# A decode layer on one core: weights loaded first in full rows, attention one kv head at a time

## The chip, the core and the metric

The kernel runs on one core of one Trainium2 chip. A core has TensorE (PE, which loads a stationary operand and streams a moving one past it), VectorE (DVE), ScalarE (ACT), GpSimd (POOL) and SyncE (SP, which here only issues transfers). Transfers between the chip's memory (HBM) and the on-chip memory (SBUF, 128 partitions) run on 16 DMA engines; products land in PSUM. The metric is the device time of one launch in microseconds (us), the median of several runs. Durations come from a profile of one execution.

## The reference

One token (x, 576 wide, bf16) is normalised. From the normalised row xn two branches are computed, and both are added to x.

```python
x = A_x                                     # 1 x 1 x 576
xn = _layernorm(x)
return x + _A_ref(xn, k_cache, v_cache, wq, wo) + _B_ref(xn, w_in, w_sp, b_sp, w_out)

# A: attention, 32 query heads, 16 kv heads, Dh = 128, the last W = 4096 of 65536 cached keys
q = xn @ wq                                 # wq 576 x 4096
p = softmax(q k^T * Dh ** -0.5)             # two query heads share one kv head
A = (p v).reshape(1, 1, 4096) @ wo          # wo 4096 x 576

# B: gated MLP at sequence length 1
z = gelu(xn @ w_in)                         # w_in 576 x 4608
z1, z2 = z[:2304], layernorm(z[2304:])
B = (z1 * (w_sp * z2 + b_sp)) @ w_out       # w_out 2304 x 576
```

All tensors are bf16. Read from HBM are K and V of 16 heads (1 MiB each, 32 MiB in all), wq and wo (4.7 MB each), w_in (5.3 MB) and w_out (2.7 MB): 51 MB, each byte once.

## The kernel before

**Loads.** All large loads are issued by SP, in program order as far as the scheduler keeps it. K, V, the eight column blocks of wq and the three chunks of w_out share one ring of 11 tiles of 8 KB per partition (`kvpool`); a load into a used tile waits until its last reader is done. `load_kn` and `load_v` (lines 114 to 121) bring a whole head as 128 partitions of 8 KB. The order is K 0 and 1, wq, K 2 and 3, w_in, V 0 to 3, K 4 to 7, w_out, V 4 to 7, K 8 to 15, wo, V 8 to 15. wq comes as blocks of 512 columns, in pieces of 1 KB:

```python
nc.sync.dma_start(t[:, 0:4, :], A_wq[0:512, 512 * bk:512 * (bk + 1)].rearrange("(kt p) c -> p kt c", p=P))
```

**x.** Three small loads on SP, then statistics over partitions with a product with ones (line 91), Ln and Exp on ACT for the reciprocal root (lines 96 and 97), and `xn_col` with xn in five columns (line 99).

**q and z.** The weights are the stationary operand and xn the moving one, one column wide: 32 x 5 products into `qps` (line 251), 36 x 5 into `zps` (line 269). GELU, the second normalisation and the gate follow as small operations on 128 x 36 (lines 278 to 316) and give `hv`.

**Attention in groups of four kv heads** (g = 0 to 3). `transpose_k` (line 124) turns a head's K into kT with 32 transposes on PE (line 131) and four copies of 128 x 1024 out of PSUM, one in three on ACT (line 133), the others on DVE (line 135). `group_scores` puts the four heads of the group on the four column groups of PE (partition rows 0, 32, 64, 96): eight chunks of 512 keys, four products each (line 148), and one Exp over 98 rows (line 156). `group_ptrans` turns the probabilities back with 32 transposes (line 170) and four copies (line 173). `group_pv` runs, head after head, 32 products of 128 x 2 by 128 x 128 on that head's column group (line 185), then scales (line 194), transposes and copies into `oT_all`.

**Output.** Products with one column of `hv` or `oT_all` as the stationary operand and rows of w_out (line 343) or wo (line 210) as the moving one, 512 and 64 columns, on two column groups. At the end wo's products of groups 0 and 1 come before V of group 2, and so on; lines 375 to 379 give this order. The sum is added to x on one partition (line 387) and stored.

The framework's scheduler chooses the order of each engine's instructions from the program order, and sets all semaphores.

Of the kernel before, what the change touches and what calls it, by code (L numbers as in the profile page):

```python
# [12 lines left out]
AXX = mybir.AxisListType.X  # L13

# [8 lines left out]
NFT = F // 128  # L23
NT = W // 128
NKC = W // 512
NGRP = 4
# [4 lines left out]
DEV_ATTN_ONLY = False  # L31
# [3 lines left out]
def kernel(  # L35
# [19 lines left out]
    ps_s = ctx.enter_context(tc.tile_pool(name="ps_s", bufs=1, space=bass.MemoryType.PSUM))  # L55
    ps_t = ctx.enter_context(tc.tile_pool(name="ps_t", bufs=4, space=bass.MemoryType.PSUM))
    ps_o = ctx.enter_context(tc.tile_pool(name="ps_o", bufs=1, space=bass.MemoryType.PSUM))
    ps_early = tc.alloc_tile_pool(name="ps_early", bufs=1, space=bass.MemoryType.PSUM)
    kvpool = ctx.enter_context(tc.tile_pool(name="kvpool", bufs=11))
    ktpool = ctx.enter_context(tc.tile_pool(name="ktpool", bufs=4))  # L60
    ppool = ctx.enter_context(tc.tile_pool(name="ppool", bufs=2))

    x_flat = A_x.flatten_outer_dims()

    ones_f = const.tile([P, P], FP32, name="ones_f")
    nc.vector.memset(ones_f[:], 1.0)
    ident = const.tile([P, P], BF16, name="ident")
    make_identity(nc, ident[:])
    eps_t = const.tile([P, 1], FP32, name="eps_t")
    nc.vector.memset(eps_t[:], EPS)  # L70

    xcol_bf = const.tile([P, 5], BF16, name="xcol_bf")
    nc.sync.dma_start(xcol_bf[:, 0:4], x_flat[0, 0:512].rearrange("(t p) -> p t", p=P))
    nc.sync.dma_start(xcol_bf[0:64, 4:5], x_flat[0, 512:576].rearrange("(t p) -> p t", p=64))
    x_row = const.tile([1, D], BF16, name="x_row")
    nc.sync.dma_start(x_row[:], x_flat)
    x_col = const.tile([P, 5], FP32, name="x_col")
    nc.vector.memset(x_col[:], 0.0)
    nc.vector.tensor_copy(x_col[:, 0:4], xcol_bf[:, 0:4])
    nc.vector.tensor_copy(x_col[0:64, 4:5], xcol_bf[0:64, 4:5])  # L80

    stat2 = const.tile([P, 2], FP32, name="stat2")
    nc.vector.reduce_sum(stat2[:, 0:1], x_col[:], axis=AXX)
    junk5 = work.tile([P, 5], FP32, name="junk5")
    nc.vector.tensor_tensor_reduce(  # L85
        out=junk5[:], in0=x_col[:], in1=x_col[:], scale=1.0, scalar=0.0,
        op0=ALU.mult, op1=ALU.add, accum_out=stat2[:, 1:2],
    )
    early_ps = ps_early.tile([P, 80], FP32, name="early_ps")
    XS = 68  # L90
    nc.tensor.matmul(early_ps[:, XS:XS + 2], lhsT=ones_f[:], rhs=stat2[:], start=True, stop=True)  # L91
    mv = const.tile([P, 4], FP32, name="mv")
    nc.vector.tensor_scalar_mul(mv[:, 0:2], early_ps[:, XS:XS + 2], 1.0 / D)
    nc.vector.tensor_mul(mv[:, 2:3], mv[:, 0:1], mv[:, 0:1])
    nc.vector.tensor_sub(mv[:, 2:3], mv[:, 1:2], mv[:, 2:3])
    nc.scalar.activation(mv[:, 2:3], mv[:, 2:3], ACT.Ln, bias=eps_t[:, 0:1])
    nc.scalar.activation(mv[:, 3:4], mv[:, 2:3], ACT.Exp, scale=-0.5)
    xn_col = const.tile([P, 5], BF16, name="xn_col")
    nc.vector.tensor_scalar(out=xn_col[:], in0=x_col[:], scalar1=mv[:, 0:1], scalar2=mv[:, 3:4],
                            op0=ALU.subtract, op1=ALU.mult)  # L100

    oT_all = const.tile([P, HQ], BF16, name="oT_all")
    sps = [ps_s.tile([P, 512], FP32, name=f"sps{b}") for b in range(2)]
    for b in range(2):
        nc.vector.memset(sps[b][:], 0.0)
    ops = ps_o.tile([P, DH], FP32, name="ops")
    nc.vector.memset(ops[:], 0.0)

    kn_tiles: dict = {}
    kT_tiles: dict = {}  # L110
    v_tiles: dict = {}
    state = {"sps": 0, "cp": 0}

    def load_kn(j):
        kn = kvpool.tile([P, NT, DH], BF16, name=f"kn{j}", tag="kv")
        nc.sync.dma_start(kn[:], A_k_cache[0, j, SK - W:SK, :].rearrange("(p t) d -> p t d", p=P))
        kn_tiles[j] = kn

    def load_v(j):
        v_sb = kvpool.tile([P, NT, DH], BF16, name=f"v_sb{j}", tag="kv")  # L120
        nc.sync.dma_start(v_sb[:], A_v_cache[0, j, SK - W:SK, :].rearrange("(p t) d -> p t d", p=P))
        v_tiles[j] = v_sb

    def transpose_k(j):
        kn = kn_tiles.pop(j)
        kT = ktpool.tile([P, NT, P], BF16, name=f"kT{j}", tag="kT")
        for q in range(NT // 8):
            tps = ps_t.tile([P, 8, P], BF16, name=f"ktps{j}_{q}", tag="tps")
            for s8 in range(8):
                t = 8 * q + s8  # L130
                nc.tensor.transpose(tps[:, s8, :], kn[:, t, :], ident[:])  # L131
            if state["cp"] % 3 == 2:
                nc.scalar.copy(kT[:, 8 * q:8 * q + 8, :], tps[:, :, :])  # L133
            else:
                nc.vector.tensor_copy(kT[:, 8 * q:8 * q + 8, :], tps[:, :, :])
            state["cp"] += 1
        kT_tiles[j] = kT

    def group_scores(g):
        p_sb = ppool.tile([P, NT, P], BF16, name=f"p_sb{g}", tag="p_sb")  # L140
        acc = work.tile([P, NKC], FP32, name=f"acc{g}", tag="acc")
        for kc in range(NKC):
            sp = sps[state["sps"] % len(sps)]
            state["sps"] += 1
            for i in range(4):
                j = 4 * g + i
                h0 = 2 * j
                nc.tensor.matmul(  # L148
                    sp[32 * i:32 * i + 2, :],
                    lhsT=q_bf[:, h0:h0 + 2],  # L150
                    rhs=kT_tiles[j][:, 4 * kc:4 * kc + 4, :],
                    start=True,
                    stop=True,
                    tile_position=(0, 32 * i),
                )
            nc.scalar.activation(  # L156
                p_sb[0:NR, 4 * kc:4 * kc + 4, :], sp[0:NR, :], ACT.Exp, scale=SCALE,
                accum_out=acc[0:NR, kc:kc + 1],
            )
        for i in range(4):  # L160
            kT_tiles.pop(4 * g + i)
        return p_sb, acc

    def group_ptrans(g, p_sb):
        ptsb = ppool.tile([P, NT, 8], BF16, name=f"ptsb{g}", tag="ptsb")
        for ti in range(NT // 8):
            ptps = ps_t.tile([P, 8, P], BF16, name=f"ptps{g}_{ti}", tag="tps")
            for s8 in range(8):
                t = 8 * ti + s8
                nc.tensor.transpose(ptps[:, s8, 0:NR], p_sb[0:NR, t, :], ident[0:NR, 0:NR])  # L170
            src = ptps[:, :, :].rearrange("p t (q r) -> p t q r", q=4)[:, :, :, 0:2]
            dst = ptsb[:, 8 * ti:8 * ti + 8, :].rearrange("p t (q r) -> p t q r", q=4)
            nc.vector.tensor_copy(dst, src)
        return ptsb

    def group_pv(g, ptsb, acc):
        asum = work.tile([P, 1], FP32, name=f"asum{g}", tag="asum")
        nc.vector.reduce_sum(asum[0:NR, :], acc[0:NR, :], axis=AXX)
        rs = work.tile([P, 1], FP32, name=f"rs{g}", tag="rs")
        nc.vector.reciprocal(rs[0:NR, :], asum[0:NR, :])  # L180
        for i in range(4):
            j = 4 * g + i
            vj = v_tiles.pop(j)
            for tt in range(NT):
                nc.tensor.matmul(  # L185
                    ops[32 * i:32 * i + 2, :],
                    lhsT=ptsb[:, tt, 2 * i:2 * i + 2],
                    rhs=vj[:, tt, :],
                    start=(tt == 0),
                    stop=(tt == NT - 1),  # L190
                    tile_position=(0, 32 * i),
                )
        on_sb = work.tile([P, DH], BF16, name=f"on_sb{g}", tag="on_sb")
        nc.vector.tensor_scalar_mul(on_sb[0:NR, :], ops[0:NR, :], rs[0:NR, :])
        otps = ps_t.tile([P, 8, P], BF16, name=f"otps{g}", tag="tps")
        nc.tensor.transpose(otps[:, 0, 0:NR], on_sb[0:NR, :], ident[0:NR, 0:NR])
        src = otps[:, 0, :].rearrange("p (q r) -> p q r", q=4)[:, :, 0:2]
        dst = oT_all[:, 8 * g:8 * g + 8].rearrange("p (q r) -> p q r", q=4)
        nc.vector.tensor_copy(dst, src)  # L199

    NCH0, NCH1 = 512, D - 512
    out_ps = [None, None]
    out_tp = [(0, 0), (0, 32)]
    out_splits = [(0, NCH0), (NCH0, NCH1)]

    def emit_wo_mms(h_lo, h_hi, wo_sb, last):
        for h in range(h_lo, h_hi):
# [28 lines left out]
    for kt in range(4):  # L236
        nc.sync.dma_start(win_sb[kt][:], B_w_in[kt * P:(kt + 1) * P, :])
# [187 lines left out]
```

## Time and profile before

| | |
|---|---|
| median of 3 runs | 151.73 us (151.55 to 153.25) |
| span of the profiled execution | 149.2 us; its own time is not listed beside it |
| mean granted TensorE clock | 0.874 |
| PE busy | 120.2 us (81%) |
| DVE, ACT busy | 41.4 us, 47.2 us |
| bytes on SP's queue | 50.96 MB, 17252 packets |
| mean rate over the span | 343 GB/s |

Busy time of PE is modelled and pipelined products overlap in it, so 81% is not a measure of how near PE is to its peak. The page cuts the span into 40 slices of 3.7 us, with the rate of the transfers in each. A stage table gives the same for stretches of one's own choice: busy time of each engine (instructions in brackets), granted clock as a share of full speed, share of the time that the DMA engines were busy, and GB/s. The chain that ended last is followed back from the end, and names at each step what released it. In a group's row stand line, engine, operation, output<-input, shapes, count, then busy us and mean ns, then idle time of the engine ahead of it and what ended it.

### The profile page before, as it was taken

What the parts mean: (1) busy time and instruction counts of PE and PEld (TensorE: products, weight loads), DVE (VectorE), ACT (ScalarE), POOL (GpSimd) and SP (SyncE); (2) the same over time, 40 slices, a digit from 0 to 9 for tenths busy, and PEclk for the clock granted to TensorE, in tenths of its full rate; (3) what the DMA queues carried; (4) which work ended last, traced back from release to release, by engine and by line L of the source; (5) the groups of instructions that cost most, each with busy time, mean ns of one, the idle gap of its engine ahead of it and who ended that gap; (6) DMA issues with size and microseconds to landing.
All of it is one profiled execution on the core that took longest, in us unless ns stands there. A gap on an engine that the chain in (4) does not pass through costs nothing. (4 is left out here: it accounts for less than half of the span.)

```text
span 149.2 us, 3824 instructions
## 1 busy us (share of the span) xinstructions
PE 120.2 (81%) x1728; PEld 94.1 (63%) x1728; DVE 41.4 (28%) x109; ACT 47.2 (32%) x94; POOL 1.9 (1%) x8
## 2 busy tenths in 40 slices
PE   0188566799840799998999999899799999969881
PEld 0187455677320699898876479686389546957850
DVE  3247000026210000431775010476169420010012
ACT  3414000024930000440558510346967970000000
POOL 4000000000000000000000000000000000000000
PEclk9999855558995555579999999999999999999999
DMA  2789999999999999999999999999999999999200
GB/s 10 277 336 308 282 285 290 366 422 418 420 348 189 402 422 422 413 413 362 359 415 417 420 415 420 415 422 413 365 357 357 373 415 415 422 413 411 121 0 0
DMA packets 17556, 51.20 MB, mean 343 GB/s; under 512 B 1858, under 2 KB 12868, under 8 KB 12868
## 3 DMA queue, kind: packets, MB, share of 16 engines
q1 hardware_dynamic: 17252, 50.96, 92.8%
q8 instruction: 13, 0.21, 0.6%
q0 software_dynamic: 288, 0.00, 0.2%
q14 instruction: 3, 0.02, 0.0%
HBM read 50.96 MB, written 0.00 MB: 342 GB/s over the span
## 5 line engine op out<-in xcount | busy, mean ns | idle before, releaser
L269 PE MATMUL early_ps<-xn_col,win_sb_242 128*128 128x1 bf16 x36 | 6.0, 166 | 4.0 <-DMA win_sb_242<-in_B_w_in_dram 4.0
L210 PE MATMUL out_t<-wo_sb,oT_all 128*1 128x64 bf16 (+1 forms) x64 | 8.2, 285 | 0.5 <-DVE oT_all L199 0.5
L269 PE MATMUL early_ps<-xn_col,win_sb_243 64*128 64x1 bf16 x36 | 6.6, 183 | 2.4 <-DMA win_sb_243<-in_B_w_in_dram 2.4
L148 PEld LDWEIGHTS <-q_bf 128*2 128x2 bf16 x128 | 3.8, 80 | 7.2 <-issue 4.0
L185 PEld LDWEIGHTS <-ptsb_546 128*2 128x2 bf16 x128 | 8.2, 96 | 0.0
L185 PEld LDWEIGHTS <-ptsb_1627 128*2 128x2 bf16 x128 | 6.9, 84 | 1.0 <-issue 0.7
L185 PEld LDWEIGHTS <-ptsb_1874 128*2 128x2 bf16 x128 | 6.9, 84 | 1.0 <-issue 0.7
L133 ACT COPY kT_422<-ktps_0_423 128x1024 bf16<-128x1024 bf16 x1 | 1.0, 1012 | 18.3 <-PE ktps_0_423 L131 18.3
L269 PE MATMUL early_ps<-xn_col,win_sb_239 128*128 128x1 bf16 x36 | 6.6, 185 | 0.0
L185 PEld LDWEIGHTS <-ptsb_1243 128*2 128x2 bf16 x128 | 6.5, 84 | 0.1
L269 PEld LDWEIGHTS <-win_sb_242 128*128 128x128 bf16 x36 | 3.7, 104 | 4.1 <-DMA win_sb_242<-in_B_w_in_dram 4.1
L285 ACT ACTIVATE th_gelu<-u_gelu 128x36 f32<-128x36 f32 x1 | 0.2, 232 | 19.1 <-DVE u_gelu L283 19.1
L269 PE MATMUL early_ps<-xn_col,win_sb_240 128*128 128x1 bf16 x36 | 5.9, 165 | 0.0
L269 PE MATMUL early_ps<-xn_col,win_sb_241 128*128 128x1 bf16 x36 | 5.9, 165 | 0.0
L269 PEld LDWEIGHTS <-win_sb_243 64*128 64x128 bf16 x36 | 3.7, 102 | 3.0 <-DMA win_sb_243<-in_B_w_in_dram 2.5
L278 DVE COPY zsb<-early_ps 128x36 f32<-128x36 f32 x1 | 0.2, 194 | 17.5 <-PE early_ps L269 17.5
L210 PEld LDWEIGHTS <-oT_all 128*1 128x1 bf16 x64 | 2.6, 81 | 3.8 <-DVE oT_all L199 0.8
L131 PEld LDWEIGHTS <-kn_122 128*128 128x128 bf16 x32 | 3.1, 137 | 2.8 <-DMA kn_122<-in_A_k_cache_dram 2.8
L258 DVE CAST q_bf<-early_ps 128x32 bf16<-128x32 f32 x1 | 0.2, 192 | 15.3 <-PE early_ps L251 15.3
L91 PE MATMUL early_ps<-stat_100,ones_f 128*128 128x2 f32 x2 | 0.6, 363 | 4.6 <-DVE stat_100 L85 4.6
L269 PEld LDWEIGHTS <-win_sb_240 128*128 128x128 bf16 x36 | 4.1, 115 | 0.0
L269 PEld LDWEIGHTS <-win_sb_239 128*128 128x128 bf16 x36 | 3.7, 103 | 0.5
(337 smaller groups left out, 299.9 us busy)
## 6 DMA issues: line engine op xcount, KB each, us to landing
wo_sb<-in_A_wo_dram SPq DMA_DIRECT2D x4, 1152.0 KB, 17.6
win_sb_239<-in_B_w_in_dram SPq DMA_DIRECT2D x1, 1152.0 KB
win_sb_240<-in_B_w_in_dram SPq DMA_DIRECT2D x1, 1152.0 KB, 14.6
win_sb_241<-in_B_w_in_dram SPq DMA_DIRECT2D x1, 1152.0 KB, 15.8
win_sb_242<-in_B_w_in_dram SPq DMA_DIRECT2D x1, 1152.0 KB
kn_122<-in_A_k_cache_dram SPq DMA_DIRECT2D x1, 1024.0 KB, 5.6
kn_124<-in_A_k_cache_dram SPq DMA_DIRECT2D x1, 1024.0 KB, 8.9
kn_150<-in_A_k_cache_dram SPq DMA_DIRECT2D x1, 1024.0 KB, 9.2
```

Of the source, the lines that this page charges most:

```text
L91: nc.tensor.matmul(early_ps[:, XS:XS + 2], lhsT=ones_f[:], rhs=stat2[:], start=True, stop=True)
L131: nc.tensor.transpose(tps[:, s8, :], kn[:, t, :], ident[:])
L133: nc.scalar.copy(kT[:, 8 * q:8 * q + 8, :], tps[:, :, :])
L148: nc.tensor.matmul(sp[32 * i:32 * i + 2, :], lhsT=q_bf[:, h0:h0 + 2], rhs=kT_tiles[j][:, 4 * kc:4 * kc + 4, :], start=True, stop=True, til ...
L185: nc.tensor.matmul(ops[32 * i:32 * i + 2, :], lhsT=ptsb[:, tt, 2 * i:2 * i + 2], rhs=vj[:, tt, :], start=(tt == 0), stop=(tt == NT - 1), t ...
L210: nc.tensor.matmul(out_ps[n], lhsT=oT_all[:, h:h + 1], rhs=wo_sb[:, h, c0:c0 + cw], start=st if DEV_ATTN_ONLY else False, stop=(last and h ...
L258: nc.vector.tensor_copy(q_bf[:], qps)
L269: nc.tensor.matmul(zps[:, t:t + 1], lhsT=win_sb[kt][0:kp, t * P:(t + 1) * P], rhs=xn_col[0:kp, kt:kt + 1], start=(kt == 0), stop=(kt == 4),)
L278: nc.vector.tensor_copy(zsb[:], zps)
L285: nc.scalar.activation(th[:], u[:], ACT.Exp, scale=-2.0 * GELU_C)
```

## The change

Nearly the whole body is rewritten.

- **Order of loads.** wq, then w_in, each as four tiles of 128 partitions and a fifth for the remaining 64 rows; then K 0, K 1, V 0, K 2, V 1 and so on, eleven at once and two more per step of the head loop; after K and V w_out (two tiles) and wo (chunks of 8, 8, 8, 5 and 3 heads) into the space that wq and w_in held. A weight tile t holds rows 4p + t, in full rows: 8 KB (wq) or 9.2 KB (w_in) per partition; the last 64 rows are cut in two halves, so that they too fill 128 partitions. w_out has nine successive rows per partition. wo keeps its rows of 1152 bytes. The ring holds K and V alone.
- **Order of instructions.** PE and SP are under a manual schedule: they run in program order. DVE, ACT and POOL stay with the scheduler. x is loaded on ACT's queue.
- **q and z.** xn is stationary (`xz`, one column of 32 filled), the weights are moving: 40 products of 512 columns for q, 60 of 384 for z, each four on the four column groups. The rows are turned into columns with 8 and 9 small products.
- **Statistics.** The reciprocal root is a power on POOL in place of Ln and Exp on ACT.
- **Attention, one kv head per step.** A head's 4096 keys are split over the four column groups: eight score products in two banks, two Exp, eight transposes of the probabilities, 32 PV products that alternate over the column groups. The sum over the four groups is done by two float32 products: `den` (the denominator) and `ot` (the output column). Step j has the transposes of K j, those of the probabilities of j - 1, the output column of j - 2, the scores of j, PV of j - 1, then two loads. Copies of kT go to DVE, the third of four to ACT.
- **Output.** w_out and wo are multiplied after the head loop, each row in four pieces of 144 columns on the four column groups; x is added on four partitions.

The diff, cut to its core (removed lines as in the listing above; what is left out are declarations, the small operations of the GELU and the renamed constants):

```diff
+KV_BUFS = 11
+WO_CHUNKS = (8, 8, 8, 5, 3)
...
+    nc.scalar.dma_start(xa[:], x_flat[0, 0:512].rearrange("(p t) -> p t", t=4))
...
+    def wrows(src, t):
+        return src[0:512, :].rearrange("(p t) c -> p t c", t=4)[:, t, :]
+
+    def whalf(src):
+        return src[512:576, :].rearrange("m (c j) -> (m c) j", c=2)
...
+    kv_order = [("k", 0)]
+    for j in range(1, HKV):
+        kv_order += [("k", j), ("v", j - 1)]
+    kv_order.append(("v", HKV - 1))
+    kv_order.reverse()
...
+    order = tc.manual_schedule(engines={PE, SP})
+    ctx.enter_context(order)
+
+    for t in range(4):
+        nc.sync.dma_start(wq_sb[t][:], wrows(A_wq, t))
+    nc.sync.dma_start(wq_h[:], whalf(A_wq))
+    for t in range(4):
+        nc.sync.dma_start(win_sb[t][:], wrows(B_w_in, t))
+    nc.sync.dma_start(win_h[:], whalf(B_w_in))
+    load_next(KV_BUFS)
...
+    def mean_rstd(stat_t, n, nm):
+        nc.tensor.matmul(ops[:, MS:MS + 2], lhsT=ones_f[:], rhs=stat_t[:], start=True, stop=True)
...
+        nc.gpsimd.tensor_tensor(mv[:, 3:4], mv[:, 2:3], mhalf[:], ALU.pow)
+        return mv
...
+    for t in range(5):
+        for b in range(2):
+            for i in range(4):
+                if t < 4:
+                    lhsT, rhs = xz[:, t, :], wq_sb[t][:, QC * i + 512 * b:QC * i + 512 * (b + 1)]
+                else:
+                    c0 = QC * (i % 2) + 512 * b
+                    lhsT, rhs = xz[:, 4 + i // 2, :], wq_h[:, c0:c0 + 512]
+                nc.tensor.matmul(
+                    sps[b][32 * i:32 * i + 32, :], lhsT=lhsT, rhs=rhs,
+                    start=(t == 0), stop=(t == 4), tile_position=(0, 32 * i),
+                )
...
+    w2pool = tc.alloc_tile_pool(name="w2pool", bufs=1, reuse_waits="tile")
...
+            for i in range(4):
+                c = 4 * b + i
                 nc.tensor.matmul(
+                    sps[b][32 * i:32 * i + 2, :], lhsT=q_bf[:, 2 * j:2 * j + 2],
+                    rhs=parts[c // 2][:, 512 * (c % 2):512 * (c % 2) + 512],
+                    start=True, stop=True, tile_position=(0, 32 * i),
                 )
...
+        for b in range(2):
+            for s in range(4):
+                for i in range(4):
+                    nc.tensor.matmul(
+                        ops[32 * i:32 * i + 2, 0:DH], lhsT=pt[:, 4 * b + s, i, :],
+                        rhs=v[:, 4 * (4 * b + i) + s, :],
+                        start=(b == 0 and s == 0), stop=(b == 1 and s == 3), tile_position=(0, 32 * i),
+                    )
...
+    for j in range(HKV + 2):
+        if j < HKV:
+            transpose_k(j)
+        if j == 0:
+            gz = z_columns()
+        if j == 1:
+            z_gate(*gz)
+        if 1 <= j <= HKV:
+            transpose_p(j - 1)
+        if j >= 2:
+            o_columns(j - 2)
+        if j < HKV:
+            scores(j)
+        if 1 <= j <= HKV:
+            pv(j - 1)
+        load_next(2)
+        if j == 10:
+            for i in range(2):
+                nc.sync.dma_start(
+                    wout_sb[i][:], B_w_out[ZC * i:ZC * (i + 1), :].rearrange("(p t) n -> p t n", t=9))
+            h0 = 0
+            for n, c in enumerate(WO_CHUNKS):
+                nc.sync.dma_start(
+                    wo_sb[n][:], A_wo[DH * h0:DH * (h0 + c), :].rearrange("(h d) n -> d h n", d=DH))
+                h0 += c
...
+    def project(lhsT, rhs, first, last):
+        for g in range(4):
             nc.tensor.matmul(
+                outp[32 * g:32 * g + 1, :], lhsT=lhsT, rhs=rhs[:, OC * g:OC * (g + 1)],
+                start=first, stop=last, tile_position=(0, 32 * g),
             )
```

More of the change, by code (lines that the diff above doesn't have):

```diff
@@ L58 @@
[L58 to L61, printed above, removed]
-    x_flat = A_x.flatten_outer_dims()
[L65 to L87, printed above, removed]
-    )
-    early_ps = ps_early.tile([P, 80], FP32, name="early_ps")
@@ L90 @@
[L90 to L107, printed above, removed]
+    wpool = tc.alloc_tile_pool(name="wpool", bufs=1)
@@ new lines @@
+    sps = [ps_fix.tile([P, 512], FP32, name=f"sps{b}") for b in range(2)]
+    ops = ps_fix.tile([P, 512], FP32, name="ops")
+    outp = ps_fix.tile([P, OC], FP32, name="outp")
+    nc.vector.memset(ops[:], 0.0)
+    nc.vector.memset(outp[:], 0.0)
+    x_col = const.tile([P, 6], FP32, name="x_col")
+    nc.vector.tensor_copy(x_col[:, 0:4], xa[:])
+    nc.vector.tensor_scalar(out=x_col[:, 4:6], in0=mask2[:], scalar1=xd[:, 0:1], scalar2=None, op0=ALU.mult)
+    stat = const.tile([P, 2], FP32, name="stat")
@@ new lines @@
+    qrow = const.tile([P, QC], BF16, name="qrow")
+    nc.vector.tensor_copy(qrow[:, 0:512], sps[0][:])
+    nc.scalar.copy(qrow[:, 512:1024], sps[1][:])
+    MQ = 288
+    for hh in range(8):
+        nc.tensor.matmul(
+            ops[:, MQ + 4 * hh:MQ + 4 * hh + 4], lhsT=qrow[:, DH * hh:DH * (hh + 1)],
+            rhs=ident[:, 0:P:32], start=True, stop=True,
+        )
+    q_bf = const.tile([P, HQ], BF16, name="q_bf")
+    nc.vector.tensor_copy(
+        q_bf[:].rearrange("p (i h) -> p i h", i=4),
+        ops[:, MQ:MQ + HQ].rearrange("p (h i) -> p i h", i=4),
+    )
@@ new lines @@
+    zps = [ps_t.tile([P, 512], FP32, name=f"zps{b}", tag="tps") for b in range(3)]
+    for t in range(5):
+        for b in range(3):
+            for i in range(4):
+                if t < 4:
+                    lhsT, rhs = xz[:, t, :], win_sb[t][:, ZC * i + ZB * b:ZC * i + ZB * (b + 1)]
+                else:
+                    c0 = ZC * (i % 2) + ZB * b
+                    lhsT, rhs = xz[:, 4 + i // 2, :], win_h[:, c0:c0 + ZB]
+                nc.tensor.matmul(
+                    zps[b][32 * i:32 * i + 32, 0:ZB], lhsT=lhsT, rhs=rhs,
+                    start=(t == 0), stop=(t == 4), tile_position=(0, 32 * i),
+                )
@@ L139, in group_scores @@
[L139 to L144, printed above, removed]
+        parts = []
+        for c in range(4):
+            tps = ps_t.tile([P, 8, P], BF16, name=f"ktps{j}_{c}", tag="tps")
+            for s in range(8):
+                nc.tensor.transpose(tps[:, s, :], kn[:, 8 * c + s, :], ident[:])
+            kT = ktpool.tile([P, 1024], BF16, name=f"kT{j}_{c}", tag="kT")
+            src = tps[:].rearrange("p a b -> p (a b)")
+            if c == 2:
+                nc.scalar.copy(kT[:], src)
+            else:
+                nc.vector.tensor_copy(kT[:], src)
+            parts.append(kT)
@@ L201 @@
[L201 to L207, printed above, removed]
-            for n, (c0, cw) in enumerate(out_splits):
-                st = (DEV_ATTN_ONLY and h == 0 and n >= 0)
-                nc.tensor.matmul(
-                    out_ps[n],
-                    lhsT=oT_all[:, h:h + 1],
-                    rhs=wo_sb[:, h, c0:c0 + cw],
-                    start=st if DEV_ATTN_ONLY else False,
-                    stop=(last and h == HQ - 1),
-                    tile_position=out_tp[n],
-                )
@@ L393, with transpose_p @@
-    nc.sync.dma_start(out.flatten_outer_dims()[:, :], res[:])
-    ps_out.release()
+                p_sb[0:NR, b, :], sps[b][0:NR, :], ACT.Exp, scale=SCALE, accum_out=acc[0:NR, b:b + 1],
+            )
+        asum = work.tile([P, 1], FP32, name=f"asum{j}", tag="asum")
+        nc.vector.reduce_sum(asum[0:NR, :], acc[0:NR, :], axis=AXX)
+        p_tiles[j] = (p_sb, asum)
+    def transpose_p(j):
+        p_sb, asum = p_tiles.pop(j)
+        ptps = ps_t.tile([P, 8, P], BF16, name=f"ptps{j}", tag="tps")
+        for b in range(2):
+            for s in range(4):
+                nc.tensor.transpose(
+                    ptps[:, 4 * b + s, 0:NR], p_sb[0:NR, b, 128 * s:128 * (s + 1)], ident[0:NR, 0:NR])
+        pt = work.tile([P, 8, 4, 2], BF16, name=f"pt{j}", tag="pt")
+        nc.vector.tensor_copy(pt[:], ptps[:].rearrange("p t (q r) -> p t q r", q=4)[:, :, :, 0:2])
+        pt_tiles[j] = pt
+        den = ps_t.tile([P, 512], FP32, name=f"den{j}", tag="tps")
+        nc.tensor.matmul(den[0:NR, 0:1], lhsT=mx_f[0:NR, 0:NR], rhs=asum[0:NR, :], start=True, stop=True)
+        rden = work.tile([P, 1], FP32, name=f"rden{j}", tag="rden")
+        nc.vector.reciprocal(rden[0:NR, :], den[0:NR, 0:1])
+        rd_tiles[j] = rden
```

392 lines of the change are left out of this document (162 added, 230 removed).

## The prediction

> **What bounds the kernel now.** I read the page's slices first, then a table of stages, then the chain that ended last. The page shows an almost full transfer queue:
>
> ```profile
> span 149.2 us, 3824 instructions
> PE 120.2 (81%) x1728; PEld 94.1 (63%) x1728; DVE 41.4 (28%) x109; ACT 47.2 (32%) x94; POOL 1.9 (1%) x8
> GB/s 10 277 336 308 282 285 290 366 422 418 420 348 189 402 422 422 413 413 362 359 415 417 420 415 420 415 422 413 365 357 357 373 415 415 422 413 411 121 0 0
> q1 hardware_dynamic: 17252, 50.96, 92.8%
> wo_sb<-in_A_wo_dram SPq DMA_DIRECT2D x4, 1152.0 KB, 17.6
> ```
>
> The reader sees 50.96 MB on one queue and a rate with plateaus and dips. The table of stages gives them (stretch, length, busy time of PE, PEld, DVE, ACT, POOL, granted clock, DMA share, GB/s):
>
> ```profile
> 14.00:26.00 12.00, 7.82 (x116) 6.38 (x116) 0.51 (x1) 0.00 (x0) 0.00 (x0) 0.65 1.11 284
> 30.00:42.00 12.00, 11.21 (x124) 7.30 (x125) 3.79 (x9) 7.41 (x18) 0.00 (x0) 0.81 1.01 420
> 44.00:46.00 2.00, 0.00 (x0) 0.00 (x0) 0.00 (x0) 0.00 (x0) 0.00 (x0) 0.70 0.99 154
> 46.00:48.00 2.00, 0.18 (x1) 0.10 (x1) 0.00 (x0) 0.00 (x0) 0.00 (x0) 0.50 1.01 214
> 48.00:50.00 2.00, 0.63 (x10) 0.58 (x11) 0.00 (x0) 0.00 (x0) 0.00 (x0) 0.50 0.94 336
> 106.00:118.00 12.00, 11.93 (x191) 9.41 (x190) 8.15 (x17) 9.20 (x20) 0.00 (x0) 1.00 1.08 357
> 120.00:136.00 16.00, 14.75 (x213) 10.39 (x212) 1.41 (x7) 2.45 (x8) 0.00 (x0) 1.00 1.01 418
> ```
>
> wq in 1 KB pieces (14 to 26 us) moves at 284 GB/s, wo in rows of 1152 bytes (106 to 118) at 357, w_in and K and V with 8 or 9 KB per partition at 420 and 418. From 44 to 50 us the stream falls off while PE does nothing: the last of w_in is awaited and K and V tiles hold the ring. Against 418 these three rows lose 2.5 us. The end, from the chain and the timeline, and the stretch in which the stream dies out:
>
> ```profile
> 121.08 20.30 DMA v_sb_1241<-in_A_v_cache_dram
> 141.43 1.96 PE ops L185 x32
> 146.22 0.68 DVE res L387
> 147.16 0.26 SPq L393 DMA_DIRECT2D out_dram<-res  x1
> 135.00:140.00 5.00, 5.00 (x87) 4.61 (x86) 0.00 (x0) 0.00 (x0) 0.00 (x0) 1.00 0.77 318
> 140.00:142.00 2.00, 1.47 (x28) 1.28 (x25) 0.00 (x0) 0.00 (x0) 0.00 (x0) 1.00 0.05 20
> ```
>
> The chain's last long piece is a transfer; what follows the last V tile takes 149.2 - 141.4 = 7.8 us. In the last two rows 1.63 MB pass, 3.9 us of work at 418, but the tile is there only at 141.4: the 16 engines do not finish together, which costs 141.4 - 138.9 = 2.5 us. So the kernel is bound by bytes, at three rates, with a hole and a long tail.
>
> **The change part by part: the stream.** The bytes stay 50.96 MB, of which wo is 4 x 1152 KB = 4.72 MB. wq becomes pieces of 8 KB (four tiles) and 4 KB, w_in 9.2 and 4.6 KB, w_out 10.4 KB; wo keeps 1152 bytes. The start:
>
> ```profile
> 0.74 0.42 SPq L73 DMA_DIRECT2D xcol_bf<-in_A_x_dram  x1
> 2.34 0.35 SPq L116 DMA_DIRECT2D kn_122<-in_A_k_cache_dram  x1
> 3.00:3.50 0.50, 0.00 (x0) 0.00 (x0) 0.00 (x0) 0.00 (x0) 0.00 (x0) 1.00 0.93 69
> 3.51 0.17 DVE L79 CAST x_col<-xcol_bf 128x4 f32<-128x4 bf16 x1 [1.21 <-DMA xcol_bf<-in_A_x_dram]
> 7.68 0.29 DVE L99 TENSOR_SCALAR xn_col<-x_col,mv 128x5 bf16<-128x5 f32 x1 [1.88 <-ACT mv L97]
> bsp<-in_B_b_sp_dram POOLq DMA_DIRECT2D x1, 0.5 KB, 6.9
> ```
>
> Three x loads stand ahead of the first K on SP; moved to ACT's queue, they let SP issue wq at 0.74 instead of 2.34, and bytes flow, 0.9 us after issue as now, from 1.7 us. Full rate 46.24 MB / 418 = 110.6 us; wo 4.72 / 357 = 13.2 us. The skew at the end I keep at 2.5 us. The same sum for the present stream (3.2 start, 16.6 for wq, 20.7 for w_out and wo, 93.0 for the rest, 2.5 hole, 2.5 skew = 138.5) falls 2.9 us short of 141.4; much of that is the uneven start with narrow wq pieces, so I carry 1.0 us over. The last chunk of wo lands at 1.7 + 110.6 + 13.2 + 2.5 + 1.0 = 129.0 us. No run shows wq or w_in with one row in four per tile (32 KB and 37 KB apart); their rate is bounded by 284 and 420, and I take 418, as the pieces are as long as K's.
>
> **Is the stream ever stopped?** SP's order is fixed: ten weight loads, eleven K and V tiles, then two per step of the head loop, each waiting for a tile that PE has read; behind a waiting load stand all later ones, w_out and wo too. The twelfth K/V tile needs head 0's transposes. Weights end at about 1.7 + 1.0 + 10.03 MB / 418 = 26.7 us, the eleven tiles (2.51 us each) at 54; PE can start head 0 near 30. That is 24 us of slack, and each later load has it too unless PE falls behind by as much.
>
> **PE per head.** Rows that give its work (start, length):
>
> ```profile
> 32.70 1.06 PE L131 MATMUL ktps_2_443<-ident,kn_150 128*128 128x128 bf16 x8
> 33.55 1.06 PE L131 MATMUL ktps_3_453<-ident,kn_150 128*128 128x128 bf16 x8
> 111.40 0.45 PE ktps_0_1710 L131 x8
> 87.45 6.59 PE ops L185 x128
> 105.42 0.39 PE sps_115 L148 x4
> 105.80 0.28 PE ptps_0_1628 L170 x4
> L91 PE MATMUL early_ps<-stat_100,ones_f 128*128 128x2 f32 x2 | 0.6, 363 | 4.6 <-DVE stat_100 L85 4.6
> L133 ACT COPY kT_422<-ktps_0_423 128x1024 bf16<-128x1024 bf16 x1 | 1.0, 1012 | 18.3 <-PE ktps_0_423 L131 18.3
> L135 DVE COPY kT_1043<-ktps_3_1074 128x1024 bf16<-128x1024 bf16 x1 | 0.7, 693 | 0.1
> L156 ACT ACTIVATE p_sb_1585<-sps_115 98x512 bf16<-98x512 f32 x4 | 2.4, 598 | 0.0
> L194 DVE TENSOR_SCALAR on_sb_2232<-ops,rs_2102 98x128 bf16<-98x128 f32 x1 | 0.4, 352 | 9.6 <-PE ops L185 9.6
> ```
>
> At full clock: K transposes 32 in 1.8 us (8 in 0.45); two packs of four scores 0.8; eight P transposes 0.56; PV 32 x 51.5 ns = 1.65 (128 in 6.59), now alternating over the four column groups, which can only shorten it if four overlap as the scores do (four in 0.39), to 0.4 at least; the two new float32 products (`den`, `ot`) between 0 and the 0.6 us of a float32 pair, I take 0.3 each. Sum 5.4 us; 4.15 with full overlap, 6.0 with neither gain; I take 4.8, the middle of the first two. A head's 2 MiB take 5.02 us. The four copies lie beside it: DVE 3 x 0.69 + 0.35 and some small ones, about 3 us; ACT 1.0 + 2 x 0.8 = 2.6. The scores of a head wait for its last copy, about 0.8 us after the last transpose; the P transposes of the head before, `den` and `ot` (1.2 us) stand between on PE and cover it. If DVE ran late by more than 0.4 us, PV and all heads behind it would move by the rest, in every step. PE starts at half clock (eight transposes in 0.85) and pays for the z columns and the z gate: PE's order is fixed, so the gate's product waits for GELU with head 0's P transposes queued behind it. I allow 13 us for the first two steps, to 43 us; 14 steps of 4.8 end at 110, two closing steps at 113. K and V are then all there (107), w_out lands near 114, and the 200 products of 144 columns wait for wo. q and z, 100 products in 25 packs of four where 340 stood, run beneath the weight stream: the half-clock start makes a pack some 0.5 us (an estimate: twice 0.39 for 512 columns, less for 384), 13 us in all, of which only w_in's last piece is left when the weights end. That holds if xn is there by about 15 us. The slowest small load above took 6.9 us and x's statistics 4.5 (3.5 to 8.0), so I expect xn by 12. They now end in a GpSimd power that stands in no row: the ACT pair it replaces lies within those 4.5 us, so it gains at most about 2 and is covered up to 3 us more; beyond that PE starts later by the rest, and 113 against the 129 of wo still hides 10 us of it.
>
> **The tail.** After wo's last three heads 12 products of 144 columns are left: 12 x 0.114 (half-clock PV, 1.4 us) at most, 0.3 if they overlap; I take 0.8. The sum over four rows of 144 is like the 98x128 one above, 0.37, hops 0.2, and the output from issue to end 149.2 - 147.16 = 2.04. Together 3.4 us, against 7.8. Span 129.0 + 3.4 = 132.4 us. The median of the runs, 151.73, is 2.5 us above the profiled span of 149.2; with the same surroundings the time is **135.0 us**, 11% below. A difference within 2% counts as no change.
>
> **A rule of the Trainium skill against this.** TensorE: Matmul & The Clock Gate, Part 4, says that transposes do not count as PE work for the clock gate, so that full clock does not engage for them. Here transposes in a row took 0.45 us per eight at 111 us, against 0.85 at 33 us, so the trace disagrees. By that rule the time would be rival 3's.
>
> **Rivals.** (1) PE becomes the bound. With the 5.4 us above plus 0.2 of waits per step: 43 + 14 x 5.6 + 3 + 200 x 58 ns (one product's spacing, as an unpacked transpose) + 2.6 = 139 us, time 141. For it: PE was busy 14.75 of 16 us in the stage from 120 us; against: that stage holds products that do not alternate column groups, and busy time counts pipelined products one over the other. 13%.
> (2) The weight rows miss the plateau. At 357 GB/s wq and w_in take 28.1 us instead of 24.0, time 139; at 284, 35.3, time 146. For it: 1 KB and 1152 bytes differ little, yet 284 and 357 differ much, so more than the length may count in wq's spaced rows. 11%. DMA: Bandwidth & Descriptors, Specifications, has line rate from 512 bytes on; by it 1 KB pieces would already be at the plateau and something else slows wq. The 357 at 1152 bytes speaks against the rule.
> (3) Slower: the clock. PE is now idle or lightly busy for 30 us and then waits in every step. If transposes ran at half clock throughout, a step is 4.8 + 1.8 + 0.56 = 7.2 us: 43 + 14 x 7.2 + 3 + 11.6 + 2.6 = 161, time 163. It decides from a step of 6.6 us on (155 us). That the clock can stay low while PE is busy:
>
> ```profile
> 50.00:60.00 10.00, 10.00 (x163) 9.12 (x160) 0.00 (x0) 0.00 (x0) 0.00 (x0) 0.50 1.01 419
> ```
>
> These were 128x1 products; at 33 us transposes themselves opened it within about 4 us. 4%.
> (4) The change does not do what it says: the load order stops somewhere, as at 44 us now, for 2.5 to 5 us: time 138 to 140. 4%.
>
> **How the numbers follow.** My forecast has 68%; the rest above. Downward, no skew and wo at 418 would save 4.4, to 130.6; two of these are unlikely together, so the low end is 131. The high end, 142, takes in rival 1, rival 4 and rival 2 at 357; left out are rival 3, rival 2 at 284 and a little more, some 12 in 100. Faster by over 2% (below 148.7) 0.93; within 2% 0.03; slower 0.04.
>
> **What would show it.** After: 410 to 420 GB/s from 2 us to about 115 without a hole, then 357; the first head's transposes near 30 us; PE waiting on K tiles by the later heads and on wo at the end; after the last transfer under 4 us. Wrong if wq's stretch stays below 400 GB/s, if SP waits for PE mid-stream, or if PE still works through heads when wo has landed.

## The result and the profile after

The changed kernel takes 136.56 us (median of 4 runs, 136.48 to 136.64) where the kernel before takes 152.23 (4 runs, 151.55 to 153.25). The ratio is 0.897, 95% interval 0.892 to 0.902: 10% faster. The forecast was 135.0 in a range of 131 to 142. The page after, the same rows as were read before:

```profile
span 134.7 us, 3783 instructions
PE 87.2 (65%) x1674; PEld 70.5 (52%) x1674; DVE 51.1 (38%) x173; ACT 38.9 (29%) x84; POOL 3.6 (3%) x11
GB/s 119 348 307 416 425 430 421 410 425 416 423 416 423 418 416 418 406 423 411 421 418 411 414 414 423 418 418 411 418 423 414 422 422 414 360 358 356 311 81 3
DMA packets 11145, 51.21 MB, mean 380 GB/s; under 512 B 1400, under 2 KB 5496, under 8 KB 5752
q1 hardware_dynamic: 10520, 50.96, 94.4%
q8 instruction: 13, 0.21, 0.7%
```

The same 50.96 MB go in 10520 packets instead of 17252. The hole in mid-stream and the stretch at 284 GB/s are gone; wo's step to some 358 GB/s remains, now at the end, and the first slices (3.4 us each), in which wq is loaded, are uneven. As a table of stages (stretch, length, busy PE, PEld, DVE, ACT, POOL, granted clock, DMA share, GB/s):

```profile
2.00:10.00 8.00, 0.00 (x0) 0.00 (x0) 0.79 (x5) 1.05 (x1) 1.48 (x4) 1.00 0.95 318
6.00:8.00 2.00, 0.00 (x0) 0.00 (x0) 0.03 (x1) 0.00 (x0) 0.00 (x0) 1.00 0.87 246
10.00:112.00 102.00, 79.57 (x1468) 64.61 (x1472) 48.44 (x161) 37.62 (x83) 1.10 (x2) 0.88 1.01 418
116.00:126.00 10.00, 3.50 (x100) 2.88 (x100) 0.00 (x0) 0.00 (x0) 0.00 (x0) 0.50 1.08 357
126.00:130.00 4.00, 1.70 (x52) 1.48 (x52) 0.00 (x0) 0.00 (x0) 0.00 (x0) 0.50 0.63 209
```

For 102 us the stream runs at 418 GB/s without a stop; from 2 to 10 us, the larger part of wq's stretch (its last load lands at 16.0), it has 318. The chain's end and the store, from the timeline:

```profile
120.82 9.72 DMA wo_308<-in_A_wo_dram
130.58 0.56 PE outp L405 x11
131.16 0.31 DVE res L422
131.50 0.65 SPq L423 DMA_DIRECT2D out_dram<-res  x1
```

The last transfer is there at 130.5 us (before: 141.4), and 134.7 - 130.5 = 4.2 us follow (before: 7.8). Of the 14.5 us between the spans, 10.9 are the stream and 3.6 the tail.

### The profile page after: what moved, and what is told of

It reads as the page before. It is cut to its first block, busy times and chain, and to the rows that moved or that the text cites. A ratio compares the mean times of both kernels' runs of the same rounds, so it can differ in the third digit from the quotient of the medians.

```text
span 134.7 us, 3783 instructions
## 1 busy us (share of the span) xinstructions
PE 87.2 (65%) x1674; PEld 70.5 (52%) x1674; DVE 51.1 (38%) x173; ACT 38.9 (29%) x84; POOL 3.6 (3%) x11
## 2 busy tenths in 40 slices
DMA packets 11145, 51.21 MB, mean 380 GB/s; under 512 B 1400, under 2 KB 5496, under 8 KB 5752
## 3 DMA queue, kind: packets, MB, share of 16 engines
q1 hardware_dynamic: 10520, 50.96, 94.4%
HBM read 50.96 MB, written 0.00 MB: 378 GB/s over the span
## 4 chain that ended last, share of the span: by engine, by line
DMA 60%; SPq 15%; PE 14%; DVE 5%; ACT 3%; issue 1%; ACTq 0%
DMA kn_1315<-in_A_k_cache_dram 16%; DMA kn_859<-in_A_k_cache_dram 15%; SPq L398 15%; DMA kn_108<-in_A_k_cache_dram 14%; DMA wq_88<-in_A_wq_dram 8%; DMA wo_308<-in_A_wo_dram 7%; PE ops L252 3%; PE sps_146 L326 1%; ACT p_583 L331 1%; ACT p_469 L331 1%; PE ktps_0_312 L309 1%; ACT p_697 L331 1%; PE ktps_0_399 L309 1%; PE ktps_1_323 L309 1%; PE ktps_2_421 L309 1%
## 5 line engine op out<-in xcount | busy, mean ns | idle before, releaser
L405 PEld LDWEIGHTS <-oT_all 128*1 128x1 bf16 x128 | 3.7, 114 | 8.6 <-issue 8.6
L169 PE MATMUL ops<-stat,ones_f 128*128 128x2 f32 x2 | 0.6, 362 | 10.4 <-DVE stat L162 10.4
L237 PEld LDWEIGHTS <-xz 128*32 128x32 bf16 x60 | 2.1, 117 | 9.5 <-issue 8.4
L243 DVE COPY zrow<-zps_232 128x384 f32<-128x384 f32 x1 | 0.6, 558 | 11.4 <-PE zps_232 L237 11.4
L252 PEld LDWEIGHTS ops<-id4f,zrow 128*128 128x128 f32 x18 | 4.4, 336 | 0.0
L309 PEld LDWEIGHTS <-kn_108 128*128 128x128 bf16 x32 | 3.3, 149 | 2.0 <-DMA kn_108<-in_A_k_cache_dram 2.0
L252 PE MATMUL ops<-id4f,zrow 128*128 128x4 f32 x18 | 4.4, 376 | 0.0
L405 PEld LDWEIGHTS <-hv 128*1 128x1 bf16 x72 | 1.8, 108 | 3.7 <-issue 3.7
L309 PEld LDWEIGHTS <-kn_110 128*128 128x128 bf16 x32 | 3.3, 148 | 0.8 <-issue 0.8
L208 PEld LDWEIGHTS <-xz 128*32 128x32 bf16 x40 | 1.3, 131 | 3.8 <-issue 2.1
L309 PEld LDWEIGHTS <-kn_1201 128*128 128x128 bf16 x32 | 1.8, 98 | 2.5 <-DMA kn_1201<-in_A_k_cache_dram 2.5
L405 PE MATMUL outp<-wout_310,hv 128*1 128x144 bf16 x36 | 1.2, 320 | 2.2 <-DMA wout_310<-in_B_w_out_dram 2.2
L405 PE MATMUL outp<-wo_305,oT_all 128*1 128x144 bf16 x32 | 1.1, 319 | 2.2 <-DMA wo_305<-in_A_wo_dram 2.2
L405 PE MATMUL outp<-wo_306,oT_all 128*1 128x144 bf16 x32 | 1.1, 318 | 2.2 <-DMA wo_306<-in_A_wo_dram 2.2
L309 PEld LDWEIGHTS <-kn_745 128*128 128x128 bf16 x32 | 1.8, 98 | 1.2 <-DMA kn_745<-in_A_k_cache_dram 1.2
L405 PE MATMUL outp<-wo_304,oT_all 128*1 128x144 bf16 x32 | 1.1, 320 | 2.0 <-DMA wo_304<-in_A_wo_dram 2.0
L309 PEld LDWEIGHTS <-kn_1429 128*128 128x128 bf16 x32 | 1.8, 98 | 1.2 <-DMA kn_1429<-in_A_k_cache_dram 1.2
L309 PEld LDWEIGHTS <-kn_973 128*128 128x128 bf16 x32 | 1.8, 98 | 1.2 <-DMA kn_973<-in_A_k_cache_dram 1.2
```

The lines of the kernel that those rows point to most:

```text
L169: nc.tensor.matmul(ops[:, MS:MS + 2], lhsT=ones_f[:], rhs=stat_t[:], start=True, stop=True)
L208: nc.tensor.matmul(sps[b][32 * i:32 * i + 32, :], lhsT=lhsT, rhs=rhs, start=(t == 0), stop=(t == 4), tile_position=(0, 32 * i),)
L237: nc.tensor.matmul(zps[b][32 * i:32 * i + 32, 0:ZB], lhsT=lhsT, rhs=rhs, start=(t == 0), stop=(t == 4), tile_position=(0, 32 * i),)
L243: nc.vector.tensor_copy(zrow[:, 0:ZB], zps[0][:, 0:ZB])
L252: nc.tensor.matmul(ops[:, MZ + 4 * t:MZ + 4 * t + 4], lhsT=zv[:, t, :], rhs=id4f[:], start=True, stop=True,)
L309: nc.tensor.transpose(tps[:, s, :], kn[:, 8 * c + s, :], ident[:])
```

## The experiments

Theory: the time is the time of the bytes, at the rate that each transfer's shape allows, plus what follows the last one; TensorE only has to stay out of the way. Main rival: TensorE's new order and packing are the gain.

**The base, twice.** The changed kernel unedited.

> The changed kernel once more, as the base for the runs beside it. Every theory: 136.5 us within 0.3.

> The changed kernel again, as the base for the three runs beside it: 136.5 us within 0.3.

Measured 136.47 and 136.44 us. Differences below are against these. The last two runs on wq and those of the ring and the store had no base beside them; the kernel before took 152.24 us there, against 152.91 and 152.27 beside the two bases.

**Three parts undone.** The loads of wq, the order of PV, the place of the first two K loads:

```diff
-        nc.sync.dma_start(wq_sb[t][:], wrows(A_wq, t))
+        nc.sync.dma_start(
+            wq_sb[k][:], A_wq[0:512, 512 * k:512 * (k + 1)].rearrange("(p t) c -> p t c", t=4))
```

> One part undone: the first 512 rows of wq come again as eight column blocks, in pieces of 1 KB. Theory (the time is the bytes' time, and pieces of 1 KB are slow): 4.19 MB at 284 instead of 418 GB/s, 14.8 instead of 10.0 us, so 141.2 us, and the stretch of wq near 284 GB/s. Some of it may hide in the uneven first 10 us: 139.5 to 141.5. Rival (the gain comes from TensorE's new order, the stream is only along for the ride): 136.5 to 137.

Measured 138.32 us (138.28 to 138.40): 1.85 slower, in the direction of the theory and far below its size. Its stage rows:

```profile
2.00:10.00 8.00, 1.50 (x4) 0.71 (x5) 2.72 (x18) 1.06 (x1) 2.05 (x5) 1.00 0.87 249
10.00:16.00 6.00, 0.86 (x2) 0.10 (x1) 0.00 (x0) 0.00 (x0) 0.00 (x0) 1.00 1.10 354
```

Pieces of 1 KB run at 354 GB/s here, as fast as wo's 1152 bytes, and not at the 284 of the kernel before. So the length of the pieces was not all that was wrong with wq; a later pair of runs takes that up. More is lost ahead of this stretch, while the small loads run too: 249 GB/s from 2 to 10 us where the changed kernel has 318.

```diff
-        for b in range(2):
-            for s in range(4):
-                for i in range(4):
+        for i in range(4):
+            for b in range(2):
+                for s in range(4):
                     nc.tensor.matmul(
                         ops[32 * i:32 * i + 2, 0:DH], lhsT=pt[:, 4 * b + s, i, :],
```

> One part undone: the 32 PV products of a head run one column group after the other, as before the change, instead of alternating. Both theories: PV goes back from 0.64 to about 1.65 us per head. Theory (TensorE has slack in every head): its step grows from 3.9 to 4.9 us, under the 5.02 us of a head's bytes, so the time stays within 0.3 us of 136.5. Rival (TensorE's packing is where the gain is): 16 x 1.0 us more, 150 to 153.

Measured 136.47 us (136.46 to 136.51), no difference. TensorE did get the work, as its busy time from 60 to 112 us shows, first in the base, then in this run:

```profile
60.00:112.00 52.00, 41.72 (x932) 35.69 (x933) 28.89 (x90) 24.59 (x55) 0.00 (x0) 1.00 1.01 417
60.00:112.00 52.00, 50.10 (x956) 44.77 (x950) 31.13 (x93) 25.52 (x57) 0.00 (x0) 1.00 1.01 417
50.18 1.12 PE ops L360 x32
54.76 1.12 PE ops L360 x32
```

8.4 us more busy time in the same stretch, the same 417 GB/s, the same end. In the chain (the last two lines are this run's), 32 PV products hold PE for 0.45 us in the changed kernel and for 1.12 here, and the heads that catch up come every 3.9 and every 4.6 us, below the 5.02 of the bytes. The cost is less than the expected 1.65 us: before the change all 32 products of a head stood on one column group, here eight stand on each of the four in turn. The rival is out for PV: this part of the packing is worth nothing in time by itself. The rest of TensorE's new order (q and z with the weights moving, one head per step, the fixed program order) was undone in no run.

```diff
+    load_next(2)
     for t in range(4):
         nc.sync.dma_start(wq_sb[t][:], wrows(A_wq, t))
...
-    load_next(KV_BUFS)
+    load_next(KV_BUFS - 2)
```

> One part undone: K 0 and K 1 are loaded ahead of the weights, as before the change; the ring has 11 tiles as in the changed kernel and TensorE's order is untouched, so q and z get their weights 5 us later and the first head starts near 34 us instead of 31. Theory (the order within the stream is worth nothing as long as it never stops): within 0.5 us of 136.5. Rival (weights first is itself a gain, since q and z stand ahead of every head): 139 to 141.5.

Measured 136.61 us (136.42 to 136.72): no difference, though the first head starts at 34.5 us instead of 31.1. That the weights come ahead of these two tiles is worth nothing in itself either.

**Why wq ran at 284.** Two runs go back towards before's transfers, from the 1 KB run: first the rows, then also the 64-row pieces.

```diff
-A_wq[0:512, 512 * k:512 * (k + 1)].rearrange("(p t) c -> p t c", t=4)
+A_wq[0:512, 512 * k:512 * (k + 1)].rearrange("(t p) c -> p t c", p=P)
```

> As the run with wq in pieces of 1 KB, but neighbouring partitions take neighbouring rows of wq (8 KB apart in memory, as before the change) instead of every fourth row (32 KB apart). x keeps its order, so wq's rows meet other entries of x than in the reference; the work is the same. The 1 KB run had about 355 GB/s in wq's stretch, not the 284 of before. Theory A (the rest of the 284 is the place of the rows): 284 GB/s for 4.19 MB, 14.8 instead of 11.8 us, about 141 us. Theory B (it is the 64-partition pieces that stood between the blocks): 355 GB/s and 138.3 us as in that run.

```diff
-    nc.sync.dma_start(wq_h[:], whalf(A_wq))
+        nc.sync.dma_start(wq_sb[k][0:64, 4, :], A_wq[512:576, 512 * k:512 * (k + 1)])
```

> wq exactly in before's transfers: eight blocks in pieces of 1 KB, neighbouring rows, each followed by a 64 KB transfer of the last 64 rows to 64 partitions (q's rows again meet other entries of x; same work). Theory A and theory B: 284 GB/s for 4.72 MB, 16.6 us instead of 13.1 in the 1 KB run, about 141.5 to 142 us; with the run above this tells A from B. Rival C (284 belongs to what else went on in before's first 28 us): 355 GB/s, 138.5 us.

Measured 138.06 and 140.00 us. Their stage rows in wq's stretch, in this order:

```profile
10.00:16.00 6.00, 1.78 (x7) 0.32 (x8) 0.70 (x3) 0.00 (x0) 0.53 (x1) 1.00 1.09 351
8.00:18.00 10.00, 1.78 (x3) 0.30 (x4) 1.11 (x6) 0.00 (x0) 0.56 (x1) 1.00 1.11 317
```

Theory A falls: the place of the rows changes nothing (351 against 354). Theory B is right in kind: with the eight 64 KB transfers to 64 partitions the rate falls to 317 and 1.9 us are lost. Two things differ in them, their size and their 64 partitions, and no run tells these apart; that their pieces are 1 KB long instead of 4 is worth some 0.2 us (0.52 MB at 354 instead of 418). So 140.0 - 136.5 = 3.5 us are shown to be the shape of wq's transfers: 1.6 to 1.9 from 1 KB to 8 KB, and 1.9 from the eight transfers.

This is not all of the start. The first 30 us of the changed kernel, of the run with wq exactly in before's transfers and of the kernel before:

```profile
0.00:30.00 30.00, 10.40 (x110) 4.27 (x110) 5.24 (x28) 2.35 (x3) 3.02 (x10) 0.82 0.94 366
0.00:30.00 30.00, 9.50 (x83) 3.37 (x87) 4.58 (x26) 1.87 (x2) 3.02 (x10) 0.98 0.95 318
0.00:30.00 30.00, 16.58 (x226) 14.27 (x226) 6.86 (x22) 5.09 (x6) 1.85 (x8) 0.79 0.93 270
```

By then the changed kernel is ahead of the one before by 30 x 96 / 418 = 6.9 us of the stream. wq's transfers make half of it, 30 x 48 / 418 = 3.4 us, or rather less, as that trace is of an execution of 140.9 us where the median is 140.0. What of the kernel before makes the other half (its later start, the K loads around wq, waits of its ring) stays open. From 30 to 60 us, where its hole lies, it has 380 GB/s against 418, another 2.7 us.

**The ring.** One size, and the step at which the output weights are issued:

```diff
-KV_BUFS = 11
+KV_BUFS = 4
...
-        if j == 10:
+        if j == 14:
```

> One size changed: 4 tiles in the K and V ring instead of 11 (w_out and wo are issued four steps later, so that they still follow K and V). Theory (the ring's cover carries the stream over TensorE's slow start, in which head 1's transposes end near 43 us): the sixth K/V load waits for them while the five tiles already under way are through at about 41 us, a hole of 3.5 us, after which TensorE keeps up: 139 to 141.5 us. Rival (TensorE follows the stream so closely that the ring's depth is not used): 136.5.

Measured 141.77 us (141.15 to 144.00; 141.63 without the slowest of the four): 5.2 to 5.3 slower, somewhat more than the theory gave. The stages and SP's timeline:

```profile
40.00:42.00 2.00, 2.00 (x22) 2.00 (x20) 1.28 (x4) 0.71 (x4) 0.00 (x0) 0.50 0.14 57
42.00:44.00 2.00, 1.10 (x12) 0.92 (x9) 1.36 (x5) 1.01 (x1) 0.00 (x0) 0.79 0.00 0
40.00:50.00 10.00, 8.72 (x168) 7.72 (x165) 6.74 (x26) 4.51 (x12) 0.55 (x1) 0.86 0.56 207
60.00:112.00 52.00, 40.35 (x856) 35.22 (x857) 27.64 (x81) 22.82 (x50) 0.00 (x0) 0.97 1.01 416
43.13 0.33 SPq L101 DMA_DIRECT2D kn<-in_A_k_cache_dram  x1
46.20 0.33 SPq L106 DMA_DIRECT2D v<-in_A_v_cache_dram  x1
```

The stream stands still until head 1's transposes free a tile at 43.1 us, then starts again with few transfers under way; from 40 to 50 us 10 x 211 / 418 = 5.0 us are lost, where the theory had counted only the 3.5 of the standstill. The hole of the kernel before looks like this one in another place. That the change closes it by leaving the ring to K and V and filling it ahead of TensorE's slow start is argued from there; no run gave the ring back to wq and w_out. More than 4 tiles are needed at the start (no depth between 4 and 11 was run); later 4 are enough (416 against 417 GB/s).

**What was left in the stream.** Two edits that the profile after suggests, and both together. x and the gate's scalars as rows, spread over the partitions by small products:

```diff
-    nc.scalar.dma_start(xa[:], x_flat[0, 0:512].rearrange("(p t) -> p t", t=4))
...
+    nc.scalar.dma_start(x_row[:], x_flat)
+    nc.scalar.dma_start(scal[:, 0:1], B_w_sp.flatten_outer_dims()[0:1, 0:1])
+    nc.scalar.dma_start(scal[:, 1:2], B_b_sp.flatten_outer_dims()[0:1, 0:1])
...
+    for t in range(4):
+        nc.tensor.matmul(ops[:, MX + t:MX + t + 1], lhsT=x_row[:, t:512:4], rhs=ones_r[:, 0:1],
+                         start=True, stop=True)
```

> One suspected cost taken away: x and the two scalars of the gate come as single rows (three packets) in place of 608 packets of 2, 4, 8 and 288 bytes; TensorE spreads them over the partitions with six small products, and x enters the final sum as a product with one. Theory (the dip to 246 to 348 GB/s between 6 and 10 us is the small packets, which take turns with the long ones on the same engines): 2 to 10 us at 400 GB/s or more instead of 318 on the mean, 8 x 80 / 418 = 1.5 us less, 134.7 to 135.4 us. Rival (the dip is the start of the stream itself): 136.3 to 136.6.

Measured 134.96 us (134.81 to 135.16), 1.5 less. wo comes next, with 32 successive rows per partition; `sel` sorts the output columns accordingly:

```diff
+        for c in range(4):
+            s0 = 128 - 8 * j - c
+            nc.tensor.matmul(
+                outp[:, MO:MO + 32], lhsT=sel[0:NR, s0:s0 + 128], rhs=on_sb[0:NR, 32 * c:32 * c + 32],
+                start=(j == 0 and c == 0), stop=(j == HKV - 1 and c == 3),
+            )
...
-                    wo_sb[n][:], A_wo[DH * h0:DH * (h0 + c), :].rearrange("(h d) n -> d h n", d=DH))
+                    wo_sb[n][:], A_wo.rearrange("(p u) n -> p u n", u=32)[:, h0:h0 + c, :])
```

> The term that the change left as it was: wo is loaded with 32 successive rows per partition (pieces of 9216, 5760 and 3456 bytes instead of 1152). For that the output columns are sorted by four float32 products per head in place of one, about 0.75 us more TensorE work per head. Theory (wo's 357 GB/s is the length of its pieces, and TensorE has slack): wo at 418, 13.2 to 11.3 us, 134.4 to 134.9 us. Rival (the rate at the end is low for another reason, or TensorE's slack is used up): 136.3 or more.

Measured 134.79 us (134.68 to 134.85), 1.65 less.

> Both edits together (x and scalars as rows, wo in long pieces). Theory: the two savings are in different stretches of one stream and add up, 132.8 to 133.8 us. Rival (the end is set by something other than the stream once wo is faster, as TensorE's 128 products of wo or the store): 134 to 135.

Measured 133.41 us (133.18 to 133.44), 3.0 less than the changed kernel; against the kernel before the ratio is 0.877 (0.874 to 0.879). Stage rows of the x run, the wo run and the joint run:

```profile
2.00:10.00 8.00, 3.15 (x23) 1.38 (x24) 2.86 (x21) 1.10 (x1) 0.55 (x1) 1.00 0.96 397
114.00:122.00 8.00, 4.85 (x112) 4.16 (x113) 0.19 (x1) 0.00 (x0) 0.00 (x0) 0.53 1.00 417
112.00:122.00 10.00, 7.37 (x214) 6.43 (x203) 1.31 (x6) 0.88 (x4) 0.00 (x0) 0.83 1.01 415
```

From 2 to 10 us the rate goes from 318 to 397 GB/s, and wo's goes from 357 to the plateau. The two add up (1.5 + 1.65 against 3.0), as they should if one stream sets the time.

**The store.**

```diff
-    nc.sync.dma_start(out_flat.rearrange("o (g n) -> (o g) n", g=4), res[0:P:32, :])
+    nc.scalar.dma_start(out_flat.rearrange("o (g n) -> (o g) n", g=4), res[0:P:32, :])
```

> One instruction moved: the store of the result goes out on ScalarE's queue instead of SyncE's. From the store's issue to the end the changed kernel takes 3.2 us, the one before 2.0. Theory (the longer end belongs to SyncE, which takes 0.65 us to issue it where before it took 0.26): 135.3 to 136.1 us. Rival (it is the four rows of 288 bytes, or lies behind the store): 136.3 to 136.7.

Measured 136.65 us (136.59 to 136.80): nothing gained.

```profile
131.42 1.12 ACTq L423 DMA_DIRECT2D out_dram<-res  x1
```

ScalarE takes 1.12 us to issue it where SyncE took 0.65. The issue is not SyncE's own burden; whether the four rows of 288 bytes or something behind the store make the end longer than before's stays open. Nor was the order at the end undone, wo last instead of V: that it makes the tail 3.6 us shorter is read from the two traces alone.

## Why the prediction was right, and where it was off

**The stream as the bound: right.** The sum had the last chunk of wo at 129.0 us; it came at 130.5. The plateau is 418 as taken, and the stream has it from 10 us on, through the end of wq and most of w_in; wo keeps 357; from 126 us the engines run out unevenly: the 0.84 MB of the last row and what follows would take 2.3 us at 357, until 128.3, so the skew is 2.2 us where 2.5 stood. One term was missing: the page counts 51.21 MB in all packets, 0.25 more than the sum, nearly all of it instructions (0.21 on q8). At 418 GB/s that is 0.6 us, part also of the 2.9 us by which the same sum fell short for the kernel before.

**The start: too small.** 1.0 us was carried over for it. From 2 to 10 us the stream had 318 instead of 418 GB/s, 1.9 us, and the run with x as rows shows 1.5 of these to be the small loads of x and the scalars, which the prediction looked at for their latency alone and not for what they take from the long transfers beside them. With 0.9 from here, 0.6 from the instructions, some 0.2 for a first byte near 1.9 instead of 1.7 us and 0.3 less skew, the 1.5 us by which wo came late are accounted for but for 0.1.

**The signs: three came up, though the mechanism was right.** The prediction called itself wrong if wq's stretch stayed below 400 GB/s. From 2 to 10 us it did, with 318; but with x as rows it has 397 with the same wq loads, so it was the small loads and not the spaced rows, and rival 2 is out by that run. SP did wait for PE in mid-stream, by its list of waits for 1.6 us at most, and the stream did not stop, as other transfers were under way. And 4.2 us followed the last transfer, not under 4.

**The gain of wq: right in the sum, wrong in its reason.** The working put the 284 GB/s on pieces of 1 KB. Pieces of 1 KB reach 351 to 354; the 64 KB transfers to 64 partitions between them bring 317; and some of the 284 is neither. The estimate held because the new kernel has none of these, which is partly luck. The rule of the Trainium skill that was weighed there (DMA: Bandwidth & Descriptors, Specifications: line rate from 512 bytes on) does not hold either: 354 at 1 KB is 15% under the plateau, and the wo run gains 1.65 us with longer pieces (the place of its rows changes too, which for wq was worth nothing).

**TensorE's step: too long, and without effect.** 4.8 us was taken for a head, 3.9 is what the chain shows where TensorE catches up (`on` of one head at 51.0 us, of the next at 54.9); PV was taken at up to 1.65 us and holds PE for 0.45, as four column groups overlap. The first two steps took until 46 us, not 43: the nine z columns alone hold PE for 4.2 us, which the allowance of 13 us named and did not price. By then two K tiles wait, and by head 9 TensorE waits for K:

```profile
34.68 4.17 PE ops L252 x18
42.48 0.77 PE ktps_3_432 L309 x8
57.61 0.45 PE ops L360 x32
59.06 0.45 PE ktps_2_885 L309 x8
101.18 0.62 PE L309 MATMUL ktps_0_1882<-ident,kn_1315 128*128 128x128 bf16 x8 [1.01 <-DMA kn_1315<-in_A_k_cache_dram]
```

Rival 1 (TensorE as the bound) is out by the run with PV group by group and by these waits, rival 3 by the row at 59 us: transposes take 0.45 us per eight in the steady stage, so the clock is up. Rival 4 did not come to pass; the ring of four shows what it would have cost.

**x: later than thought, still covered.** xn was expected by 12 us; the two x loads took 4.6 and 8.6 us to land, and the first q product ran at 12.6.

**The tail: 4.2 us instead of 3.4.** The twelve products took 0.6 where 0.8 stood, the sum 0.31; the store 134.7 - 131.5 = 3.2 where 2.04 was carried over from a single row of 1152 bytes. That term was mis-sized by 1.2 us. Against it the surroundings of the span are 136.56 - 134.7 = 1.9 us instead of 2.5. The 2.5 set the median of the runs against the span of another execution; where time and span of the same one are listed, the kernel before too has 1.7 to 1.8 (151.54 and 149.8). Together: 1.5 + 0.8 - 0.6 = 1.7 us, the distance to the measured 136.56 up to rounding. That the time came within 1.6 us is thus in part errors that offset each other.

## What to carry to other kernels

Where a table of stages shows the transfers busy throughout, take the time apart by their shapes before anything else: long pieces over all 128 partitions, a few rows in place of hundreds of small packets, and a ring deep enough for the slowest start were worth whole microseconds each, while 8 us of TensorE busy time added in the steady stage cost nothing. A slow rate has more than one cause: undo the suspected one by itself, since the sum can come out right for a wrong reason.

## What the runs showed of the hardware

Small packets cost far more than their bytes. 608 packets (320 on q0 and 288 on q10), of some 3.3 KB together, cost 1.5 us of a stream of 418 GB/s, the transfer time of 0.6 MB. Taking turns explains little of it: from 2 to 10 us the packets of q0 and q10 fill 2.4, 2.6, 5.8 and 8.1% of the engines' time in the four stretches of 2 us, 0.4 us together. How the rest arises stays open; a wait of SP for one of the small loads (3.4 us, before it issues more of w_in) goes away with them too.

Half clock outlasted 10 us of uninterrupted TensorE work. First the changed kernel, then the joint run, the same stretch:

```profile
32.00:42.00 10.00, 10.00 (x74) 9.14 (x72) 4.03 (x11) 2.40 (x6) 0.00 (x0) 0.50 1.01 419
32.00:42.00 10.00, 10.00 (x73) 9.13 (x72) 4.18 (x11) 2.40 (x6) 0.00 (x0) 1.00 1.01 420
```

The prediction had transposes opening the clock within about 4 us, and so it was in the kernel before: its first transposes start at 7.95 us at 0.85 us per eight, and from 11.67 on eight take 0.45. Here PE is busy for all of the 10 us, with transposes, scores and float32 products, and eight transposes still take 0.77 us or more at 42 us. Whether the float32 products do not count is not shown; no run leaves them out. The Trainium skill (TensorE: Matmul & The Clock Gate, Part 1) gives about 3.4 us of sustained work for full clock; this stretch disagrees, the steady stage does not. The second row also warns of the column: the joint run is granted full clock by it, yet does the same number of instructions in the same 10 us. The spacing of like products is the safer clock.
